# Weight assembly through PSUM, and a ring of two banks for both products of the feed-forward

## The chip, the cores and the metric

The kernel runs on one core of a Trainium2 chip. A core has TensorE (PE, matrix products into PSUM), VectorE (DVE), ScalarE (ACT), GpSimd (POOL) and the DMA queues, most of which SyncE (SP) issues to. PSUM has eight banks of 128 partitions x 512 fp32. The metric is the device time of one execution in microseconds; lower is better.

## The reference, cut to what matters

```python
# attention: B=4, H=8, S=576, D=64; only the 32 largest scores of a row are kept
scores = q @ k.T / sqrt(64)
kth    = np.partition(scores, -32)[..., -32]
attn   = softmax(where(scores >= kth, scores, -1e9))
x      = concat_heads(attn @ v)                       # 2304 tokens x 512
# feed-forward: w_in 512 x 2048, w_out 2048 x 512
h = x @ w_in
g = where(h > 0, h, exp(min(h, 0)) - 1)
y = g @ w_out
# experts: each token goes to the one of 8 whose embedding is most alike
e   = argmax(normalised(y) @ normalised(expert_emb).T / tau)
out = gate * (relu(y @ w1[e]) @ w2[e])
```

## The kernel before

**Stages.** `attention_and_ffn` does the attention, the feed-forward and the choice of the expert for all 2304 tokens; it ends at about 930 us of the trace. Then the experts follow one by one. The change touches the first part alone.

**Tiles and slots.** A tile is 128 query rows of one head (or 64 rows of two heads for the last rows of a batch); there are 144, in the order of `tiles`. Eight of them, all heads of the same 128 tokens, make a slot; there are 18 slots. A tile goes through: scores on PE into one of two `sc` banks pairs (L781), a copy by ACT into one of five `arena` buffers of a pair of tiles (L787), the search for the 32nd largest score on DVE (L676 to L708; L703 reads the `sc` bank again and so frees it), masking and exponentials on ACT and POOL (L806 to L825), a transposing DMA (L827) and the product with v on PE into the one `acc` bank (L857). After the last tile of a slot, L889 on DVE divides by the row sums, from `acc` into one of three `rr` buffers, and a DMA turns the slot's tokens into `xt`.

**Feed-forward of a slot** (`ffn_ops`, L908). The 2048 hidden columns are done in four units of 512. A unit has 48 products of 128 columns into the bank `hp` (L916 to L918), an exponential and a relu on ACT into an `rr` buffer (L938, L939), L940 on DVE, which reads `hp` and `rr`, and two copies of the result as fp16 high and low part into a buffer `gt` (L943 or L945, L946). Then come 12 products of 512 columns from `gt` into the bank `y` (L923 to L925), which collects all four units. `hp` and `y` have one bank each, `gt` has two buffers. When all is in `y`, ACT copies it out (L962), and `route_ops` finds the expert.

**Weights** (`weights`, L1105). w_in and w_out are read as halves of eight pieces each, 32 halves in all (`w_piece`, L468). Every number of a half is put together on DVE as an integer in three operations over 512 columns: c0 (L481) keeps and shifts one word into `fi`, a view of the final place in SBUF; c1 (L484) ors the sign and exponent bits of the same word into `fi`; c2 (L487) ors the shifted other word into `fi`. c1 and c2 so read two SBUF operands, the loaded words with a step of two, and `fi`. ACT sums the squares (L490), `pow2` makes a scale, and `w_split` (L499) splits each piece into a high and a low fp16 part: for w_in ACT and POOL, for w_out ACT (L507) and DVE (L512). The last piece of w_out lies in a buffer of its own, `wl`.

**Order.** A planner (`Plan`, L69) writes the order of each engine's instructions down ahead of time. Each operation has a guessed length, a due time counted in tiles, and the buffers that it reads and writes; a `Ring` hands out buffers in turn, and a ring with `in_order` only in the order in which they were asked for. The planner goes through simulated time and always puts the operation with the earliest due time next among those that can start. On the chip each engine keeps that order and waits on semaphores. First products of a unit are due at `d`, second products at `d + 2.4`; each set is cut into four operations:

```python
r_h = ring(ps, [128, 512], F32, "hp", 1)
r_y = ring(ps, [128, DM], F32, "y", K["yb"])
r_gt = ring(ff, [128, 2, 4, 128], F16, "gt", K["gt"])
d = d0 + (d1 - d0) * f / (NFB // 4)
for i in range(0, 4, n):
    FIRST["last"] = op("pe", 645 * n, d + K["f15"], lambda i=i: f2(gt, f, i, i + n), ...)
```

The bank `misc` is one as well; the transposes of q and k, `pow2` and `route_ops` use it.

Of the kernel before, what the change touches and what calls it, by code (L numbers as in the profile page):

```python
# [29 lines left out]
K = {'WD': 2.5, 'wa': 0.7, 'ws': 6.0, 'wsa': 0.6, 'wo': 6.0, 'wos': 13.0, 'wsp': (1, 1, 1, 1, 1, 1, 1, 1, 0, 0, 0, 0, 0, 0, 0, 0), 'kd': 5, 'qd': 7, 'vs': 1.3, 'va': 0.25, 'vp': -5.0, 'u': 20, 'cut': 4, 'ff0': 7, 'ffd': 7.0, 'rr': 3, 'nj': (3, 1), 'big': 3, 'kt': 4, 'wt': 0.4, 'wf': 0.9, 'vpo': 0, 'gth': 2, 'a4': (0, 20, 1), 'hp': 2, 'yb': 1, 'sc': 3, 'xt': 2, 'xsp': 0, 's': 5, 'w': 1, 'gt': 2, 'qraw': 1, 'dsc': 3.5, 'dcp': 2.0, 'dsg': 0.2, 'drl': 1.0, 'de': 1.0, 'dex': 0.8, 'dhi': 0.8, 'dlo': 0.9, 'dav': 3.5, 'dno': 3.5, 'drt': 2.0, 'f3': 0.3, 'f6': 0.6, 'f9': 0.9, 'f15': 2.4, 'ffs': 0.0, 'ct': 0.4, 'we': 0, 'wd0': -2.9, 'ahead': 4}  # L30
# [159 lines left out]
def topk_attention_ffn_experts_kernel(  # L190
# [160 lines left out]
    def attention_and_ffn(fast):  # L351
# [116 lines left out]
        def w_piece(t, tb, i, src, st, stb, due, far=()):  # L468

            f = wview(t, i, 2)  # L470
            k = src.shape[1] // 2
            for h in range(2):
                d = far[(2 * i + h) % len(far)] if far else r_big()
                fh = f[:, h * 512:(h + 1) * 512]
                fi = fh.bitcast(I32)
# [20 lines left out]
                if h:
                    op("act", 1040, due + 1, sq, r=[tb[i + 1]], w=[d, stb])

        def w_split(t, tb, i, sb, due, pool):  # L499
# [408 lines left out]
        def ffn_ops(c, d0, d1):  # L908
            xt, y = xts[c], r_y()
# [10 lines left out]
            def f2(gt, f, i0, i1):  # L920
                for i in range(i0, i1):
                    fb = 4 * f + i
                    nc.tensor.matmul(y.t, gt.t[:, 0, i, :], wo_at(0, fb), start=(fb == 0), stop=False)  # L923
# [111 lines left out]
        def first_expert():  # L1035
# [463 lines left out]
```

## Time and profile before

| | |
|---|---|
| median of 3 runs | 1254.1 us (1249.03 to 1255.2) |
| profiled execution, device time | 1257.39 us |
| its span, first to last instruction | 1255.6 us |
| mean granted TensorE clock | 0.913 |
| busy in the span | PE 83%, DVE 69%, ACT 68%, POOL 62% |
| DMA | 165.85 MB, 132 GB/s mean |

Times in the rows are counted from the first instruction of the span. The device time is 1.8 us longer than the span. Busy shares are means over stages that differ, so the rows below take the stages one by one. Matmuls overlap each other, and a product's length in the trace is its latency; how fast PE goes is read from the distance of two starts. The granted clock is a share of 2.4 GHz.

### The profile page before, as it was taken

How to read it: one execution, taken by the hardware profiler on the slowest of the kernel's cores; microseconds unless marked ns; L12 is line 12 of the kernel's file. 1: busy time of each engine (PE TensorE's matmuls, PEld its weight loads, DVE VectorE, ACT ScalarE, POOL GpSimd, SP SyncE). 2: the span in 40 equal slices, each digit the busy share in tenths (PEclk: the TensorE clock that was granted, in tenths of full speed). 3: DMA queues.
4: the chain of work that ended last, by engine and by line, in shares of the span. 5: the costliest groups of instructions: out<-in, count | busy, mean ns of one | idle time of the engine just before them, and what ended most of it. 6: DMA issues, size and time to landing. Idle time of an engine off the chain costs nothing. (4 is left out here: it accounts for less than half of the span.)

```text
span 1255.6 us, 28591 instructions
## 1 busy us (share of the span) xinstructions
PE 1036.1 (83%) x10112; PEld 799.0 (64%) x10112; DVE 865.1 (69%) x3588; ACT 847.8 (68%) x1807; POOL 780.8 (62%) x816
## 2 busy tenths in 40 slices
PE   4565537899798999798898988998887788998996
PEld 2354426666566777576676666776664677777785
DVE  4789999988798988789887898886213244434310
ACT  3687878889788989878887888876233244444421
POOL 1267979887688988678886788988313234323300
PEclk9957757999899999989998988999898889999998
DMA  7997633746764757945756674434407455455400
GB/s 202 303 235 192 161 93 71 144 94 149 161 122 100 125 107 156 167 81 102 126 95 127 146 145 85 90 77 89 136 11 228 143 184 185 134 163 178 142 20 16
DMA packets 321732, 165.85 MB, mean 132 GB/s; under 512 B 257990, under 2 KB 298054, under 8 KB 321552
## 3 DMA queue, kind: packets, MB, share of 16 engines
q1 hardware_dynamic: 316816, 150.67, 52.1%
q0 software_dynamic: 4736, 12.92, 3.4%
q8 instruction: 95, 1.56, 0.6%
q14 instruction: 85, 0.70, 0.2%
HBM read 77.43 MB, written 11.40 MB: 71 GB/s over the span
## 5 line engine op out<-in xcount | busy, mean ns | idle before, releaser
L916 PE MATMUL hp<-xt,ww 128*128 128x128 f16 x1152 | 216.8, 229 | 25.0 <-DVE rr L940 22.8
L917 PE MATMUL hp<-xt,ww 128*128 128x128 f16 x1152 | 216.7, 229 | 0.0
L918 PE MATMUL hp<-xt,ww 128*128 128x128 f16 x1152 | 216.4, 229 | 0.0
L816 POOL TENSOR_TENSOR arena<-arena,k 128x576 f32<-128x576 f32 x144 | 191.4, 1330 | 37.6 <-ACT k L806 36.7
L825 POOL TENSOR_TENSOR php<-arena,php 128x576 f16<-128x576 f32 x144 | 188.0, 1306 | 6.5
L781 PE MATMUL sc<-arena_r,qd 128*128 128x288 bf16 (+1 forms) x960 | 145.5, 308 | 43.2 <-ACT arena L787 17.7
L676 DVE MAX8 cand<-arena 128x8 f32<-128x82 f32 (+1 forms) x1008 | 161.3, 229 | 26.1 <-ACT arena L787 25.2
L787 ACT ACTIVATE arena<-sc 128x288 f32<-128x288 f32 x288 | 113.5, 408 | 47.0 <-PE sc L781 45.4
L857 PEld LDWEIGHTS <-pt 128*128 128x128 f16 (+3 forms) x2400 | 99.7, 104 | 68.6 <-DMA pt<-php 36.3
L781 PEld LDWEIGHTS <-qd 128*128 128x128 bf16 (+1 forms) x960 | 86.7, 107 | 88.4 <-issue 44.7
L916 PEld LDWEIGHTS <-ww 128*128 128x128 f16 x1152 | 119.8, 104 | 27.1 <-DVE rr L940 15.3
L821 POOL TENSOR_SCALAR php<-arena 128x576 f16<-128x576 f32 x144 | 101.5, 705 | 47.4 <-ACT arena L818 44.3
L917 PEld LDWEIGHTS <-ww 128*128 128x128 f16 x1152 | 118.8, 103 | 17.1 <-issue 11.9
L691 ACT ACTIVATE k<-arena,mba 128x576 bf16<-128x576 f32 x144 | 111.4, 774 | 14.8 <-DVE mx L696 7.7
L806 ACT ACTIVATE k<-arena,mba 128x576 bf16<-128x576 f32 x144 | 111.7, 776 | 14.0 <-DVE mba L708 8.0
L818 ACT ACTIVATE arena<-arena,mx 128x576 f32<-128x576 f32 x144 | 111.6, 775 | 11.8 <-POOL arena L816 11.4
L918 PEld LDWEIGHTS <-ww 128*128 128x128 f16 x1152 | 119.0, 103 | 0.0
L857 PE MATMUL acc<-vb,pt 128*128 128x64 f16 (+1 forms) x1920 | 91.5, 201 | 32.7 <-DMA pt<-php 30.8
L925 PE MATMUL y<-ww,gt 128*128 128x512 f16 x288 | 109.2, 379 | 4.6 <-POOL gt L946 4.6
L707 DVE MAX8 w<-w 128x8 f32<-128x585 f32 x144 | 109.9, 763 | 4.1 <-POOL w L701 3.2
L923 PE MATMUL y<-ww,gt 128*128 128x512 f16 x288 | 109.5, 380 | 0.6 <-ACT gt L945 0.6
L924 PE MATMUL y<-ww,gt 128*128 128x512 f16 x288 | 109.1, 379 | 0.0
(300 smaller groups left out, 2747.1 us busy)
## 6 DMA issues: line engine op xcount, KB each, us to landing
arena<-in_moe_w_dram SPq DMA_DIRECT2D x52, 512.0 KB, 5.6
arena_r<-big SPq DMA_DIRECT2D x64, 144.0 KB, 2.6
big<-in_moe_w_out_dram SPq DMA_DIRECT2D x16, 512.0 KB, 4.6
ww<-in_moe_w_in_dram SPq DMA_DIRECT2D x14, 512.0 KB, 7.1
qd<-big SPq DMA_DIRECT2D x32, 192.0 KB, 2.9
ysc<-big SPq DMA_DIRECT2D x20, 258.0 KB, 4.8
w<-in_moe_w_dram SPq DMA_DIRECT2D x10, 512.0 KB, 12.4
big<-in_v_dram SPq DMA_DIRECT2D x9, 512.0 KB, 8.8
```

Of the source, the lines that this page charges most:

```text
L676: v.max(out=cand.t[:, 8 * g:8 * g + 8], in_=x()[:, ENDS[g]:ENDS[g + 1]])
L691: op("act", 760, n + K["dsg"], lambda: nc.scalar.activation(k.t(), x(), AF.Sign, scale=-1.0, bias=th.t, accum_out=ds.t), r=[sb, th, k.base ...
L781: nc.tensor.matmul(o[64 * g:64 * g + 64] if s is None else o, qd.t[:, i, g, p * n:p * n + n], kt.t[:, g, i // 2, cs], start=i == 0, stop=i ...
L787: op("act", 291, n - K["dcp"], lambda c=c: nc.scalar.activation(sb.t()[:, c * 288:c * 288 + 288], sc.t[:, SC0 + c * 288:SC0 + c * 288 + 28 ...
L806: op("act", 667, n + K["drl"], lambda: nc.scalar.activation(k.t(), sb.t(), AF.Relu, scale=-HUGE, bias=kb.t), r=[sb, kb, s2, k2], w=[k])
L816: op("pool", 1242, e, lambda sb_=sb_, k_=k_: nc.gpsimd.tensor_tensor(sb_.t(), sb_.t(), k_.t(), op=ALU.subtract), r=[k_, s2, k2], w=[sb_])
L818: op("act", 760, e + K["dex"], lambda sb_=sb_, mx_=mx_, i_=i_: nc.scalar.activation(sb_.t(), sb_.t(), AF.Exp, scale=scale, bias=mx_(), acc ...
L825: op("pool", 1270, e + K["dlo"], lambda sb_=sb_, i=i: nc.gpsimd.tensor_tensor(ph.t[:, i, 1, 0:S], sb_.t(), ph.t[:, i, 0, 0:S], op=ALU.subt ...
L857: nc.tensor.matmul(acc.t[out_, cs], t[h][rows, g, :], rhs, start=(i == 0), stop=(i == len(units) - 1))
L916: nc.tensor.matmul(hp.t[:, i * 128:i * 128 + 128], wi_at(0, kb, fb), xh, start=(kb == 0), stop=False)
L917: nc.tensor.matmul(hp.t[:, i * 128:i * 128 + 128], wi_at(0, kb, fb), xl, start=False, stop=False)
L918: nc.tensor.matmul(hp.t[:, i * 128:i * 128 + 128], wi_at(1, kb, fb), xh, start=False, stop=(kb == KB - 1))
```

## The change

**Assembly.** Each half takes a PSUM bank `x`, from the ring `hp` for w_in and from `misc` for w_out. c0 writes to `x`, c1 reads and writes `x`, and c2 reads `x` and writes the final place in SBUF. The planner's guesses go from 400, 700, 700 to 400, 600, 600 ns.

**Banks of the feed-forward.** The ring `y` goes, and `hp` has two banks. A slot takes five turns of that ring: four units, and then `y`. The second products of a slot are no longer put behind each unit but all together behind the fourth, due at the end of the slot's time (`d1`). So `gt` has four buffers: two as before, two as views of `wl`. The first copy into `gt` of each unit has to wait for the last split that reads `wl` (`done`).

```diff
@@ K @@
-'gt': 2
+'gt': 4
@@ rings @@
-        r_h = ring(ps, [128, 512], F32, "hp", 1)
-        r_y = ring(ps, [128, DM], F32, "y", K["yb"])
+        r_h = ring(ps, [128, 512], F32, "hp", 2)
...
-        r_gt = ring(ff, [128, 2, 4, 128], F16, "gt", K["gt"])
+        gts = [ff.tile([128, 2, 4, 128], F16, name=f"gt{i}", bufs=1) for i in range(2)]
+        gts += [wl.bitcast(F16)[:, i * 1024:i * 1024 + 1024].rearrange("p (a b c) -> p a b c", a=2, b=4) for i in range(2)]
+        r_gt = turns(4, lambda i: gts[i])
@@ w_piece @@
-                fh = f[:, h * 512:(h + 1) * 512]
-                fi = fh.bitcast(I32)
+                x = (r_h if t is wi else r_misc)()
+                fi = f[:, h * 512:(h + 1) * 512].bitcast(I32)
...
-                def c0(d=d, fi=fi):
-                    nc.vector.tensor_scalar(fi, d.t[:, 0:1024].bitcast(I32)[:, 1:1024:2], 0x07FFFFFF, 3, op0=ALU.bitwise_and, op1=ALU.logical_shift_left)
+                def c0(d=d, x=x):
+                    nc.vector.tensor_scalar(x.t.bitcast(I32), d.t[:, 0:1024].bitcast(I32)[:, 1:1024:2], 0x07FFFFFF, 3, op0=ALU.bitwise_and, op1=ALU.logical_shift_left)
-                def c1(d=d, fi=fi):
-                    nc.vector.scalar_tensor_tensor(fi, d.t[:, 0:1024].bitcast(I32)[:, 1:1024:2], -0x40000000, fi, op0=ALU.bitwise_and, op1=ALU.bitwise_or)
+                def c1(d=d, x=x):
+                    nc.vector.scalar_tensor_tensor(x.t.bitcast(I32), d.t[:, 0:1024].bitcast(I32)[:, 1:1024:2], -0x40000000, x.t.bitcast(I32), op0=ALU.bitwise_and, op1=ALU.bitwise_or)
-                def c2(d=d, fi=fi):
-                    nc.vector.scalar_tensor_tensor(fi, d.t[:, 0:1024].bitcast(I32)[:, 0:1024:2], 29, fi, op0=ALU.logical_shift_right, op1=ALU.bitwise_or)
+                def c2(d=d, x=x, fi=fi):
+                    nc.vector.scalar_tensor_tensor(fi, d.t[:, 0:1024].bitcast(I32)[:, 0:1024:2], 29, x.t.bitcast(I32), op0=ALU.logical_shift_right, op1=ALU.bitwise_or)
...
-                op("dve", 400, due, c0, r=[d], w=[tb[i + 1]])
-                op("dve", 700, due, c1, r=[d], w=[tb[i + 1]])
-                op("dve", 700, due, c2, r=[d], w=[tb[i + 1]])
+                op("dve", 400, due, c0, r=[d], w=[x])
+                op("dve", 600, due, c1, r=[d], w=[x])
+                op("dve", 600, due, c2, r=[d, x], w=[tb[i + 1]])
@@ w_split: the same operation, and done[:] = [it] @@
@@ get_q: the first q's bank @@
-            x, m, qn, qd, qx = r_qraw(), (r_misc if QT else r_y)(), r_big(), r_qd(), Buf(t=1)
+            x, m, qn, qd, qx = r_qraw(), (r_misc if QT else r_h)(), r_big(), r_qd(), Buf(t=1)
@@ ffn_ops @@
-            xt, y = xts[c], r_y()
+            xt, second = xts[c], []
...
-                    op("act", 520, d + K["f9"], lambda: nc.scalar.activation(gt.t[:, 0], v3(r.t), AF.Copy), r=[r], w=[gt])
+                    op("act", 520, d + K["f9"], lambda: nc.scalar.activation(gt.t[:, 0], v3(r.t), AF.Copy), r=[r], w=[gt], after=done)
...
-                for i in range(0, 4, n):
-                    FIRST["last"] = op("pe", 645 * n, d + K["f15"], lambda i=i: f2(gt, f, i, i + n), r=[gt] + wo_b[2 * f + i // 2:2 * f + (i + n + 1) // 2], w=[y])
+                second.append((gt, f))
 
             for f in range(NFB // 4):
                 unit(f)
+            y, n = r_h(), 4 // K["cut"]
+            for gt, f in second:
+                for i in range(0, 4, n):
+                    FIRST["last"] = op("pe", 645 * n, d1 + (f - 3) * .2, lambda gt=gt, f=f, i=i: f2(y, gt, f, i, i + n),
+                                       r=[gt] + wo_b[2 * f + i // 2:2 * f + (i + n + 1) // 2], w=[y])
@@ first_expert: two banks of hp in place of hp and y @@
-            up0(op, N + 60, x0, x, [r_h(), r_y()], late(0, 1024), Buf(t=1), raw, after=[FIRST["last"]])
+            up0(op, N + 60, x0, x, [r_h(), r_h()], late(0, 1024), Buf(t=1), raw, after=[FIRST["last"]])
```

## Rows read from the trace of the kernel before

**Rows 1.** Busy tenths of the page, 40 slices of 31.4 us: VectorE.

```profile
DVE  4789999988798988789887898886213244434310
```

**Rows 2.** Busy us by stretch: length, PE, PEld, DVE, ACT, POOL; clock, DMA share, GB/s.

```profile
150.00:200.00 50.00, 23.13 (x216) 16.89 (x214) 49.83 (x174) 39.01 (x74) 43.00 (x33) 0.62 0.33 83
400.00:500.00 100.00, 96.92 (x1162) 71.97 (x1160) 89.69 (x421) 91.17 (x214) 88.72 (x102) 1.00 0.59 118
```

**Rows 3.** Timeline of PE, second products of a slot: start us, length us.

```profile
889.04 0.38 PE L924 MATMUL y<-ww,gt 128*128 128x512 f16 x1
889.26 0.38 PE L925 MATMUL y<-ww,gt 128*128 128x512 f16 x1
```

**Rows 4.** Groups by line, DVE, 86 to 176 us: busy us, mean ns, idle before.

```profile
L484 DVE SCALAR_TENSOR_TENSOR ww<-big,ww 128x512 int32<-128x512 int32 x14 | 18.0, 1284 | 0.0
L487 DVE SCALAR_TENSOR_TENSOR ww<-big,ww 128x512 int32<-128x512 int32 x14 | 14.8, 1059 | 0.0
L481 DVE TENSOR_SCALAR ww<-big 128x512 int32<-128x512 int32 x14 | 12.9, 921 | 0.0
```

**Rows 5.** The same groups by line, DVE, 25 to 80 us.

```profile
L487 DVE SCALAR_TENSOR_TENSOR ww<-ww 128x512 int32<-128x512 int32 x14 | 12.9, 935 | 0.0
L484 DVE SCALAR_TENSOR_TENSOR ww<-ww 128x512 int32<-128x512 int32 x14 | 10.7, 782 | 0.0
L481 DVE TENSOR_SCALAR ww<-ww 128x512 int32<-128x512 int32 x14 | 9.0, 661 | 2.3 <-DMA ww<-in_moe_w_in_dram 2.3
```

**Rows 6.** One line each: count, ns least/median/most, first and last start us.

```profile
L484 DVE SCALAR_TENSOR_TENSOR ww<-big,ww x14: 672/1276/2480, 87.3 to 165.1; 128x512 int32<-128x512 int32 x14
L481 DVE TENSOR_SCALAR ww<-ww x14: 407/416/1498, 26.6 to 68.9; 128x512 int32<-128x512 int32 x14
L940 DVE SCALAR_TENSOR_TENSOR rr<-hp,sc,rr x4: 723/739/751, 188.7 to 221.9; 128x512 f32<-128x512 f32 x4
L703 DVE SCALAR_TENSOR_TENSOR w<-sc,mba,arena x115: 767/810/819, 234.6 to 849.1; 128x576 f32<-128x576 f32 x115
```

**Rows 7.** Groups by line, POOL: L816 in 86 to 176, then 230 to 850 us.

```profile
L816 POOL TENSOR_TENSOR arena<-arena,k 128x576 f32<-128x576 f32 x10 | 15.2, 1516 | 3.3 <-ACT k L806 2.9 <-ACT big L527 0.4
...
L816 POOL TENSOR_TENSOR arena<-arena,k 128x576 f32<-128x576 f32 x116 | 149.1, 1287 | 25.3 <-ACT k L806 24.7
```

**Rows 8.** One line each, as in rows 6: last weight split, first g, second slot's normalisation.

```profile
L512 DVE SCALAR_TENSOR_TENSOR ww<-wl,so,ww x1: 2261/2261/2261, 209.2 to 209.2; 128x1024 f16<-128x1024 f32 x1
L943 POOL TENSOR_SCALAR gt<-rr x18: 609/620/647, 189.5 to 907.3; 128x512 f16<-128x512 f32 x18
L889 DVE TENSOR_TENSOR rr<-acc,rinv x1: 667/667/667, 197.4 to 197.4; 128x512 f32<-128x512 f32 x1
```

**Rows 9.** Waits, 230 to 850 us: us in total, times, longest.

```profile
ACT arena L787 <- PE sc L781: 33.9, 39, 3.8
PE sc L781 <- DVE w L703: 6.9, 7, 1.5
PE hp L916 <- DVE rr L940: 6.7, 7, 1.6
```

**Rows 10.** Last slot: its stretch, then timelines of ACT and DVE (start, length us).

```profile
897.90:929.10 31.20, 27.52 (x253) 21.33 (x254) 4.69 (x14) 8.28 (x14) 6.87 (x9) 0.84 0.03 10
904.89 0.69 ACT L938 ACTIVATE rr<-hp,sc 128x512 f32<-128x512 f32 x1 [0.63 <-PE hp L918]
911.77 0.69 ACT L938 ACTIVATE rr<-hp,sc 128x512 f32<-128x512 f32 x1 [5.34 <-PE hp L918]
922.31 0.69 ACT L938 ACTIVATE rr<-hp,sc 128x512 f32<-128x512 f32 x1 [2.23 <-PE hp L918]
929.06 0.69 ACT L962 ACTIVATE big<-y,sc 128x512 f32<-128x512 f32 x1 [3.66 <-PE y L925]
906.46 0.75 DVE L940 SCALAR_TENSOR_TENSOR rr<-hp,sc,rr 128x512 f32<-128x512 f32 x1 [1.73 <-ACT rr L939]
918.61 0.75 DVE L940 SCALAR_TENSOR_TENSOR rr<-hp,sc,rr 128x512 f32<-128x512 f32 x1 [4.52 <-ACT rr L939]
```

More of the change, by code (lines that the diff above doesn't have):

```diff
@@ L29 @@
 ENDS = (0, 83, 166, 248, 330, 412, 494, 576)
-K = {'WD': 2.5, 'wa': 0.7, 'ws': 6.0, 'wsa': 0.6, 'wo': 6.0, 'wos': 13.0, 'wsp': (1, 1, 1, 1, 1, 1, 1, 1, 0, 0, 0, 0, 0, 0, 0, 0), 'kd': 5, 'qd': 7, 'vs': 1.3, 'va': 0.25, 'vp': -5.0, 'u': 20, 'cut': 4, 'ff0': 7, 'ffd': 7.0, 'rr': 3, 'nj': (3, 1), 'big': 3, 'kt': 4, 'wt': 0.4, 'wf': 0.9, 'vpo': 0, 'gth': 2, 'a4': (0, 20, 1), 'hp': 2, 'yb': 1, 'sc': 3, 'xt': 2, 'xsp': 0, 's': 5, 'w': 1, 'gt': 2, 'qraw': 1, 'dsc': 3.5, 'dcp': 2.0, 'dsg': 0.2, 'drl': 1.0, 'de': 1.0, 'dex': 0.8, 'dhi': 0.8, 'dlo': 0.9, 'dav': 3.5, 'dno': 3.5, 'drt': 2.0, 'f3': 0.3, 'f6': 0.6, 'f9': 0.9, 'f15': 2.4, 'ffs': 0.0, 'ct': 0.4, 'we': 0, 'wd0': -2.9, 'ahead': 4}
+K = {'WD': 2.5, 'wa': 0.7, 'ws': 6.0, 'wsa': 0.6, 'wo': 6.0, 'wos': 13.0, 'wsp': (1, 1, 1, 1, 1, 1, 1, 1, 0, 0, 0, 0, 0, 0, 0, 0), 'kd': 5, 'qd': 7, 'vs': 1.3, 'va': 0.25, 'vp': -5.0, 'u': 20, 'cut': 4, 'ff0': 7, 'ffd': 7.0, 'rr': 3, 'nj': (3, 1), 'big': 3, 'kt': 4, 'wt': 0.4, 'wf': 0.9, 'vpo': 0, 'gth': 2, 'a4': (0, 20, 1), 'hp': 2, 'yb': 1, 'sc': 3, 'xt': 2, 'xsp': 0, 's': 5, 'w': 1, 'gt': 4, 'qraw': 1, 'dsc': 3.5, 'dcp': 2.0, 'dsg': 0.2, 'drl': 1.0, 'de': 1.0, 'dex': 0.8, 'dhi': 0.8, 'dlo': 0.9, 'dav': 3.5, 'dno': 3.5, 'drt': 2.0, 'f3': 0.3, 'f6': 0.6, 'f9': 0.9, 'f15': 2.4, 'ffs': 0.0, 'ct': 0.4, 'we': 0, 'wd0': -2.9, 'ahead': 4}
 def pick(n, key):
@@ L415, in attention_and_ffn @@
         r_pw = ring(sm, [128, 4], F32, "pw", 1)
-        for r in [r_sc, r_s, r_k, r_php, r_pt, r_top, r_w, r_acc, r_xs, r_xt, r_h, r_gt, r_y]:
+        for r in [r_sc, r_s, r_k, r_php, r_pt, r_top, r_w, r_acc, r_xs, r_xt, r_h, r_gt]:
             r.in_order = True
@@ L511, in w_split @@
                 return
-            op("dve", 1196, due, lambda: nc.vector.scalar_tensor_tensor(lo, f, s, hi, op0=ALU.mult, op1=ALU.subtract),
-               r=[tb[i + 1], sb], w=[tb[i]])
+            done[:] = [op("dve", 1196, due, lambda: nc.vector.scalar_tensor_tensor(lo, f, s, hi, op0=ALU.mult, op1=ALU.subtract),
+               r=[tb[i + 1], sb], w=[tb[i]])]
         def wi_at(part, kb, fb):
@@ L519, in wo_at @@
             return wview(wo, fb // 2, part)[:, (fb % 2) * 512:(fb % 2) * 512 + 512]
-        KT, VB, QT, hold = {}, {}, {}, []
+        KT, VB, QT, hold, done = {}, {}, {}, [], []
         def thirds(x, m, first, due, dst, ns, reads):
@@ L918, in f1, with f2 @@
                         nc.tensor.matmul(hp.t[:, i * 128:i * 128 + 128], wi_at(1, kb, fb), xh, start=False, stop=(kb == KB - 1))
-            def f2(gt, f, i0, i1):
+            def f2(y, gt, f, i0, i1):
                 for i in range(i0, i1):
@@ L942, in unit @@
                 if (4 * c + f) * K["gth"] % 8 < K["gth"]:
-                    op("pool", 588, d + K["f9"], lambda: nc.gpsimd.tensor_scalar(gt.t[:, 0], v3(r.t), 1.0, 0.0, op0=ALU.mult, op1=ALU.add), r=[r], w=[gt])
+                    op("pool", 588, d + K["f9"], lambda: nc.gpsimd.tensor_scalar(gt.t[:, 0], v3(r.t), 1.0, 0.0, op0=ALU.mult, op1=ALU.add), r=[r], w=[gt], after=done)
                 else:
-                    op("act", 520, d + K["f9"], lambda: nc.scalar.activation(gt.t[:, 0], v3(r.t), AF.Copy), r=[r], w=[gt])
+                    op("act", 520, d + K["f9"], lambda: nc.scalar.activation(gt.t[:, 0], v3(r.t), AF.Copy), r=[r], w=[gt], after=done)
                 op("pool", 1113, d + K["f9"], lambda: nc.gpsimd.tensor_tensor(gt.t[:, 1], v3(r.t), gt.t[:, 0], op=ALU.subtract), r=[r], w=[gt])
-                for i in range(0, 4, n):
-                    FIRST["last"] = op("pe", 645 * n, d + K["f15"], lambda i=i: f2(gt, f, i, i + n), r=[gt] + wo_b[2 * f + i // 2:2 * f + (i + n + 1) // 2], w=[y])
+                second.append((gt, f))
             for f in range(NFB // 4):
                 unit(f)
+            y, n = r_h(), 4 // K["cut"]
[3 more added lines that the diff above has]
+                                       r=[gt] + wo_b[2 * f + i // 2:2 * f + (i + n + 1) // 2], w=[y])
             route_ops(c, y, d1 + K["drt"])
```

## The prediction

> **What bounds the kernel now.** I read the busy tenths of the page first. VectorE (DVE) stands at 7 to 9 from slice 2 to slice 27 (a slice is 31.4 us) and at 4 or less after slice 28, where the attention ends [rows 1]. Next comes the table by stretch: from 150 to 200 us DVE is busy 49.83 of 50 us, PE 23.13 at a granted clock of 0.62; from 400 to 500 us PE 96.92, ACT 91.17, DVE 89.69 and POOL 88.72 of 100 [rows 2]. PE's figure flatters: two second products start 0.22 us apart and last 0.38 each, so its busy time is no measure of room left [rows 3]. So the kernel has a start in which DVE is full and PE is not, a middle in which all are nearly full, and an expert part. The start is a DVE queue: what is taken off DVE there moves all later work forward, while the middle has no single owner.
>
> Third, what DVE does in its full stretch, 86 to 176 us: the three integer operations that assemble w_out, 18.0 + 14.8 + 12.9 us for 14 of 16 half-pieces, so 3.26 us each and about 52 us for 16, of 90 [rows 4]. For w_in (25 to 80 us) the same three cost 12.9 + 10.7 + 9.0 us for 14, 2.33 each, 37 us for 16 [rows 5]. The reason is in the spread: L484 ran at 672 ns least, 1276 median and 2480 most over w_out's pieces, whereas L940, which has as many elements but one operand in PSUM, took 723 to 751 just afterwards, and L703, also with a PSUM operand, 767 to 819 over the whole middle [rows 6]. POOL pays too: its subtraction L816 took 1516 ns in 86 to 176 us against 1287 later [rows 7]. DVE and POOL delay each other when DVE takes two SBUF operands, as L484 and L487 do.
>
> **The assembly through PSUM.** Nothing is added or dropped: 3 operations x 32 half-pieces stay. c1 and c2 keep one SBUF operand and get one from PSUM; c0 and c1 write to PSUM. The page "GPSIMD Engine Reference" of the Trainium skill (Specifications) says that POOL shares its SBUF interface with DVE instructions that have two SBUF inputs or run in a two-port mode; rows 6 agree.
>
> - c2 has exactly the pattern of L940: 0.74 us [rows 6].
> - c1 also writes PSUM, which no row shows for this size. Bounds: 0.67 (the SBUF form undisturbed) and 0.82 (the longest L703, 576 columns instead of 512) [rows 6]. I take 0.74, as L940 is nearest.
> - c0 undisturbed takes 407 to 416 ns [rows 6], faster than one element per cycle of its neighbours. Bounds 0.41 and 0.82 as above; I take 0.67, the undisturbed time of the one-element rate, because one end of it is now PSUM.
>
> The rule that speaks against the change is here: "VectorE: DVE Perf Modes" of the Trainium skill (Why PSUM operands drop a tier) says that an fp32 operation with a PSUM operand runs at one element per cycle. By it the fast c0 is lost, and the sum stays as it is below; were it not so, another 8 us would go. No row shows this operation into PSUM.
>
> Sum per half: 0.67 + 0.74 + 0.74 = 2.15 us (1.82 to 2.38). For w_out 3.26 - 2.15 = 1.11 us, x 16 = **17.8 us** off a saturated DVE (14 to 23). For w_in 2.33 - 2.15 = 0.18 x 16 = 2.9 us (-1 to 8); there part of the time goes to loads and short waits, and I count it as 0. I take 17 for both, a little less than the first, because the halves share one bank (below). POOL's shorter times in the same stretch are cover for DVE's gain, no separate term.
>
> Banks: w_in's halves use the two hp banks, idle at that time. w_out's use the one misc bank, which the q transposes and the scale of w_out also want. A half holds it for its three operations, which run on one engine anyhow; a q or k preparation can push a half back, but DVE then has tile work. Cost 0; at worst a few us, inside the lower bound above.
>
> **The wait on the weight split.** All first copies of g now wait for the last L512. That starts at 209.2 and takes 2.26 us, so it ends at 211.5; before, the first copy started at 189.5 [rows 8]. With the start 17 us shorter it is 194.5 against 172.5. Queued behind: the second products of slot 0, and, less visibly, the three rr buffers, which units 0 to 2 then hold; the normalisation of slot 1 (197.4 [rows 8], so 180) needs one, holds the only acc bank, and could be 14 us late. What hides it: DVE works at the front of the attention, and the outputs of a tile are due 3.5 tiles later; it is full anyhow. I take 0; without that cover it is up to 14 us.
>
> **The second hp bank and the second products at the end of a slot.** The work is the same: 4 x 48 first and 48 wide products per slot. What goes is PE's wait for L940 before the next unit: 6.7 us in 7 times over the 620 us of the middle, of which the other engines hide most; ACT's 33.9 us for scores is a much larger wait and remains [rows 9]. Gain in the middle between 0 and 7 us; I take 0. What is late next: y now takes a turn in the same ring, so five allocations per slot go over two banks, and unit 1 of the next slot waits until ACT has copied y out.
>
> At the end of the attention nothing covers the wait, and the last slot shows it. The last slot begins at 897.9 us at a clock of 0.84 and y is copied out at 929.06 [rows 10]. Now: unit 0's first products end at 904.9, L940 at 906.46 + 0.75 = 907.2, only then unit 1, done at 911.8 (4.6 us, below full clock); unit 3 takes from 919.4 to 922.3 (2.9 us) [rows 10]. After: unit 1 follows at once, 904.9 + 4.6 = 909.5; unit 2 needs only L940 of unit 0, 912.4; unit 3's bank is free at 909.5 + 2.3 = 911.8, so it ends at 915.3. Then 48 wide products x 0.22 [rows 3] = 10.6 us: 925.9, with g of unit 3 ready in time (its L940 ends 917.6, PE comes to it at 923.2). That is 3.2 us sooner; if unit 1 too runs in 2.9, 4.9. I take **4 us** (0 to 8).
>
> **The sum.** The profiled execution took 1257.4 us (its span 1255.6 and 1.8 around it), 3.3 above the median of 1254.1. 17 + 4 = 21 us less: 1236.4 by the profile, **1233** against the median. The rest of the program has no date of its own: each step waits for earlier steps, so a forward shift goes through to the end.
>
> **The rivals.**
>
> 1. *The middle shortens too.* PE's 6.7 us go with everything queued behind them, w_in's 2.9 come through, and c0 keeps its fast rate, (0.67 - 0.41) x 32 = 8: 1233 - 18 = 1215. For it: PE and DVE are both near 90% in 400 to 500 us [rows 2], where small jitters add up. Against it: the wait is small beside those for scores.
> 2. *The start's gain is given back.* c0 and c1 near 0.82, so 17 becomes 14, and slot 0's 14 us wait for rr stalls the back of the attention, which the middle cannot make up: 1254 - 4 = 1250. For it: DVE's 49.83 of 50 says nothing about whether the outputs, not DVE, end each stage. Against it: five pairs of score buffers lie between.
> 3. *Slower: the block of second products holds up the scores.* 16 pieces, 10.6 us of PE, now fall due together, and the scores of a tile can only begin when L703 has freed one of two sc banks (PE already waited 6.9 us for that [rows 9]). DVE has one tile in hand, some 5 us (the 115 L703 come one in 5.4 us [rows 6]); if the planned order puts more than that in front of a score, DVE stands still. Place: the join of two slots, 15 times. At 2.5 us each that is 38 us: 1233 + 38 = 1271. It decides from 1.4 us per slot (21 / 15). For it: the order is fixed ahead by estimated times. Against it: the products are cut in pieces and overdue scores are placed first.
>
> **How the numbers follow.** Forecast 0.61 (its own range 1222 to 1245), rival 1 0.14, rival 2 0.13, rival 3 0.12. Range 1212 to 1252: all of the forecast, most of rivals 1 and 2, none of 3. A difference under 0.5% (6.3 us) is no change for this measurement: faster than 1247.8 are the forecast, rival 1 and a quarter of rival 2, 0.78; same most of rival 2, 0.11; slower rival 3, 0.11.
>
> **What would show it.** L481, L484 and L487 at 0.67, 0.74 and 0.74 with little spread, and L816 near 1.29 us in the start: the first step. The last L512 some 17 us earlier, and every later eviction of y too: that the gain goes through. L889 of slot 1 not before the last L512: the rr wait. First products of units 0 and 1 of the last slot back to back: the tail. The prediction is wrong if the evictions of y lose the 17 us on the way, or if DVE's wait for scores grows at slot joins.

## The result and the profile after

The changed kernel takes 1232.3 us in the median of 4 runs (1226.75 to 1234.84) against 1253.0 for the kernel before. The ratio is 0.984, 95% interval 0.9814 to 0.9867. The profiled execution took 1234.8 us, its span is 1233.0, so the span is 22.6 us shorter. The interval leaves no doubt of a gain, though it is under 2%. Lines have moved: c0, c1, c2 are L485, L488, L491, the last split is L516, L676 is now L680, L703 is L707, L707 is L711, L781 and L787 are L785 and L791, L816 is L820, L889 is L893, L916 is L920, L938 and L940 are L942 and L944, L943 is L947, and the copy of y L962 is L970. In the experiments, one of the nine runs of e6_done23, the longest at 1246.2 us, counts as slow and is left out of its ratio.

The busy tenths of the page after, VectorE, 40 slices, now of 30.8 us:

```profile
DVE  4789898998779897798789889987113443334310
```

By stretch (length, then busy us of PE, PEld, DVE, ACT, POOL, then clock, DMA share, GB/s):

```profile
86.00:162.00 76.00, 44.88 (x472) 34.95 (x472) 69.61 (x268) 67.96 (x133) 61.58 (x49) 0.72 0.74 190
150.00:200.00 50.00, 25.75 (x230) 19.90 (x230) 47.05 (x191) 43.58 (x85) 44.18 (x37) 0.63 0.39 84
400.00:500.00 100.00, 94.95 (x1149) 71.19 (x1146) 88.51 (x423) 92.14 (x217) 84.21 (x97) 0.98 0.71 130
```

and the kernel before over its own stretch of the same work, the assembly of w_out:

```profile
86.00:176.00 90.00, 49.02 (x460) 37.10 (x459) 88.96 (x285) 70.23 (x139) 70.91 (x50) 0.69 0.68 166
```

DVE was busy 88.96 of 90 us there and is now busy 69.61 of 76: it has some room [rows 2]. The middle, 400 to 500 us, looks as before.

The three assembly operations, one line each (count, ns least/median/most, first and last start). The rows with misc as bank are w_out's, those with hp w_in's:

```profile
L485 DVE TENSOR_SCALAR misc<-big x16: 670/682/695, 87.1 to 158.7; 128x512 int32<-128x512 int32 x16
L485 DVE TENSOR_SCALAR hp<-ww x14: 671/686/695, 26.5 to 72.0; 128x512 int32<-128x512 int32 x14
...
L488 DVE SCALAR_TENSOR_TENSOR misc<-big,misc x16: 675/684/697, 88.7 to 160.0; 128x512 int32<-128x512 int32 x16
L488 DVE SCALAR_TENSOR_TENSOR hp<-ww,hp x14: 674/692/697, 27.2 to 72.8; 128x512 int32<-128x512 int32 x14
...
L491 DVE SCALAR_TENSOR_TENSOR ww<-ww,hp x14: 664/680/686, 28.4 to 73.5; 128x512 int32<-128x512 int32 x14
L491 DVE SCALAR_TENSOR_TENSOR ww<-big,misc x14: 656/677/686, 89.4 to 154.8; 128x512 int32<-128x512 int32 x14
```

No row is above 697 ns. Before, the same operations ran up to 2480 [rows 6]. All 32 halves took 88.0 us of DVE, summed over the trace, and now take 65.6, 2.05 per half.

POOL's subtraction in the same stretch (busy us, mean ns, idle):

```profile
L820 POOL TENSOR_TENSOR arena<-arena,k 128x576 f32<-128x576 f32 x9 | 11.5, 1282 | 5.3 <-ACT k L810 4.7 <-DVE pw L448 0.6
```

It is back at about its length of the middle [rows 7].

The last weight split, the first copies of g and the second slot's division, as in [rows 8]:

```profile
L516 DVE SCALAR_TENSOR_TENSOR ww<-wl,so,ww x1: 1284/1284/1284, 194.9 to 194.9; 128x1024 f16<-128x1024 f32 x1
...
L947 POOL TENSOR_SCALAR gt<-rr x18: 608/618/674, 197.9 to 890.7; 128x512 f16<-128x512 f32 x18
...
L893 DVE TENSOR_TENSOR rr<-acc,rinv x2: 676/679/682, 201.1 to 228.7; 128x512 f32<-128x512 f32 x2
```

The split ends at 196.2 us instead of 211.5, 15.3 sooner. The first L947 starts at 197.9, behind it. Of the two L893 the first belongs to the second slot: 201.1 us, later than before (197.4), though everything around it comes sooner.

Waits from 215 to 830 us (us in total, times, longest):

```profile
ACT arena L791 <- PE sc L785: 48.1, 36, 5.6
DVE cand L680 <- ACT arena L791: 20.5, 22, 4.3
PE sc L785 <- DVE w L707: 4.6, 7, 1.3
PE hp L920 <- DVE rr L944: 3.6, 3, 1.4
```

PE's wait for L944 before the next unit went from 6.7 to 3.6 us [rows 9]; ACT waits more for scores, 48.1 us against 33.9, and DVE waits 20.5 us for ACT's copies of them, twice as long as before (230 to 850 us):

```profile
DVE cand L676 <- ACT arena L787: 10.4, 18, 1.4
```

The last slot: its stretch, then ACT's timeline (start, length), with the copy of y of the slot ahead and of the last:

```profile
884.00:907.00 23.00, 22.89 (x245) 17.27 (x245) 3.00 (x4) 7.93 (x12) 5.24 (x5) 0.94 0.01 3
```

```profile
875.19 0.69 ACT L970 ACTIVATE big<-hp,sc 128x512 f32<-128x512 f32 x1 [6.81 <-PE hp L929]
888.31 0.69 ACT L942 ACTIVATE rr<-hp,sc 128x512 f32<-128x512 f32 x1 [6.75 <-PE hp L922]
890.93 0.69 ACT L942 ACTIVATE rr<-hp,sc 128x512 f32<-128x512 f32 x1 [1.09 <-PE hp L922]
893.82 0.67 ACT L942 ACTIVATE rr<-hp,sc 128x512 f32<-128x512 f32 x1
896.69 0.67 ACT L942 ACTIVATE rr<-hp,sc 128x512 f32<-128x512 f32 x1
906.73 0.69 ACT L970 ACTIVATE big<-hp,sc 128x512 f32<-128x512 f32 x1 [7.03 <-PE hp L929]
```

From the first L920 at 884.1 to the last L970 at 906.7 it takes 22.6 us; before it was 31.2 (897.9 to 929.06 [rows 10]). The exponentials come 2.6 to 2.9 us apart, where there were 6.9, 5.3 and 5.3.

**Three stages.** The sum can be read from three marks of each kernel: the end of the last weight split, the end of the last tile's search (last L707 or L711), and the last slot. The two rows of the second mark, before and after:

```profile
L707 DVE MAX8 w<-w x144: 746/762/772, 25.1 to 863.8; 128x8 f32<-128x585 f32 x144
```

```profile
L711 DVE MAX8 w<-w x144: 744/761/773, 25.4 to 850.2; 128x8 f32<-128x585 f32 x144
```

| | split ends | middle, to the last search | last slot | span |
|---|---|---|---|---|
| before | 211.5 | 653.1 | 31.2 | 1255.6 |
| changed | 196.2 | 654.8 | 22.6 | 1233.0 |

15.3 us came in the start, -1.7 in the middle, 8.6 in the last slot; the rest of the span differs by 0.4. At the split's end 20 of the 144 searches were done before and 21 are now (20 to 22 in all kernels below), so the first mark stands at nearly the same work. Each trace is one execution, and the timed executions of one kernel lie 2 to 17 us apart here: a single stage's difference of a few microseconds is not clear of that.

### The profile page after: what moved, and what is told of

Its sections match the earlier page's. It is cut to its first block, busy times and chain, and to the rows that moved or that the text cites. A ratio compares the mean times of both kernels' runs of the same rounds, so it can differ in the third digit from the quotient of the medians.

```text
span 1233.0 us, 28591 instructions
## 1 busy us (share of the span) xinstructions
PE 1028.0 (83%) x10093; PEld 789.9 (64%) x10093; DVE 842.7 (68%) x3588; ACT 845.8 (69%) x1807; POOL 767.8 (62%) x816
## 5 line engine op out<-in xcount | busy, mean ns | idle before, releaser
L920 PE MATMUL hp<-xt,ww 128*128 128x128 f16 x1152 | 206.8, 224 | 14.0 <-DVE rr L944 8.9
L820 POOL TENSOR_TENSOR arena<-arena,k 128x576 f32<-128x576 f32 x144 | 186.0, 1294 | 49.3 <-ACT k L810 47.8
L921 PE MATMUL hp<-xt,ww 128*128 128x128 f16 x1152 | 206.5, 223 | 0.0
L922 PE MATMUL hp<-xt,ww 128*128 128x128 f16 x1152 | 206.2, 223 | 0.0
L680 DVE MAX8 cand<-arena 128x8 f32<-128x82 f32 (+1 forms) x1008 | 161.5, 229 | 38.0 <-ACT arena L791 37.2
L785 PE MATMUL sc<-arena_r,qd 128*128 128x288 bf16 (+1 forms) x960 | 149.6, 316 | 41.5 <-ACT arena L791 16.8
L791 ACT ACTIVATE arena<-sc 128x288 f32<-128x288 f32 x288 | 113.2, 408 | 68.5 <-PE sc L785 66.5
L785 PEld LDWEIGHTS <-qd 128*128 128x128 bf16 (+1 forms) x960 | 87.2, 109 | 84.7 <-issue 38.3
L921 PEld LDWEIGHTS <-ww 128*128 128x128 f16 x1152 | 115.1, 100 | 12.3 <-issue 8.8
L920 PEld LDWEIGHTS <-ww 128*128 128x128 f16 x1152 | 115.7, 100 | 11.1 <-DVE rr L944 5.9
L825 POOL TENSOR_SCALAR php<-arena 128x576 f16<-128x576 f32 x144 | 97.6, 678 | 39.1 <-ACT arena L822 31.5
L922 PEld LDWEIGHTS <-ww 128*128 128x128 f16 x1152 | 115.2, 100 | 0.0
L711 DVE MAX8 w<-w 128x8 f32<-128x585 f32 x144 | 109.8, 763 | 2.7 <-POOL w L705 1.9
L707 DVE SCALAR_TENSOR_TENSOR w<-sc,mba,arena 128x576 f32<-128x576 f32 x124 | 100.6, 811 | 0.2
L690 DVE MAX8 top<-cand 128x8 f32<-128x56 f32 x432 | 89.2, 211 | 3.4
L1334 DVE SCALAR_TENSOR_TENSOR hl<-hp,hh 128x256 fp32r<-128x256 f32 x56 | 23.2, 422 | 97.5 <-ACT hh L1333 97.5
```

The source lines that it names most:

```text
L680: v.max(out=cand.t[:, 8 * g:8 * g + 8], in_=x()[:, ENDS[g]:ENDS[g + 1]])
L785: nc.tensor.matmul(o[64 * g:64 * g + 64] if s is None else o, qd.t[:, i, g, p * n:p * n + n], kt.t[:, g, i // 2, cs], start=i == 0, stop=i ...
L791: op("act", 291, n - K["dcp"], lambda c=c: nc.scalar.activation(sb.t()[:, c * 288:c * 288 + 288], sc.t[:, SC0 + c * 288:SC0 + c * 288 + 28 ...
L820: op("pool", 1242, e, lambda sb_=sb_, k_=k_: nc.gpsimd.tensor_tensor(sb_.t(), sb_.t(), k_.t(), op=ALU.subtract), r=[k_, s2, k2], w=[sb_])
L920: nc.tensor.matmul(hp.t[:, i * 128:i * 128 + 128], wi_at(0, kb, fb), xh, start=(kb == 0), stop=False)
L921: nc.tensor.matmul(hp.t[:, i * 128:i * 128 + 128], wi_at(0, kb, fb), xl, start=False, stop=False)
```

## The experiments

Each was timed beside the kernel before on the same chip, and not all on one chip. Ratios are to that kernel, so two experiments are compared by their ratios; the 95% interval stands in brackets.

**Assembly alone (e1_assembly).**

```diff
 r_h = ring(ps, [128, 512], F32, "hp", 1)     # as before, and r_y, two gt buffers, f2 behind each unit
+x = (r_h if t is wi else r_misc)()           # c0, c1, c2 and their guesses as in the change
```

> The kernel before with the assembly in PSUM alone (hp for w_in, misc for w_out; one hp bank, one y bank, two gt buffers, second products behind each unit as before). Theory (the gain is DVE time in the start, which passes through to the end): the three operations near 0.68 us each as in the changed kernel, the last split of w_out 12 to 17 us earlier than at 209 us, the last slot still 29 to 33 us long, time 1235 to 1240, so 13 to 18 us less than before. Rival (the feed-forward's order carries the gain and the start's time is given back in the middle): 1246 to 1253.

1225.7 us (1222.9 to 1226.9), ratio 0.981 (0.9778 to 0.9842): 24.7 us less than the kernel before, more than either theory said. Whether it is faster than the whole change (0.9814 to 0.9867) is not clear, since the intervals overlap. Its last split and its last search:

```profile
L513 DVE SCALAR_TENSOR_TENSOR ww<-wl,so,ww x1: 1750/1750/1750, 196.1 to 196.1; 128x1024 f16<-128x1024 f32 x1
...
L708 DVE MAX8 w<-w x144: 747/762/772, 25.0 to 835.8; 128x8 f32<-128x585 f32 x144
```

and ACT's timeline of its last slot:

```profile
874.25 0.69 ACT L939 ACTIVATE rr<-hp,sc 128x512 f32<-128x512 f32 x1
881.12 0.69 ACT L939 ACTIVATE rr<-hp,sc 128x512 f32<-128x512 f32 x1 [5.34 <-PE hp L919]
898.42 0.69 ACT L963 ACTIVATE big<-y,sc 128x512 f32<-128x512 f32 x1 [3.66 <-PE y L926]
```

The start (197.9) and the last slot (30.6 us) are as the theory had them. The surprise is the middle: 836.6 - 197.9 = 638.7 us, 14 less than before, with the feed-forward of the kernel before.

**Feed-forward alone (e2_ffn).**

```diff
 r_h = ring(ps, [128, 512], F32, "hp", 2)     # and all else of ffn_ops as in the change
-x = (r_h if t is wi else r_misc)()           # w_piece and its guesses as before
```

> The changed kernel with the old assembly in SBUF: two hp banks, four gt buffers, second products together, but w_piece and its guesses as before. Theory: the last slot lasts 22 to 25 us instead of 31, all else as before, time 1245 to 1249. Rival (the feed-forward's order carries the gain): 1233 to 1240. Second rival (the block of second products costs the middle more than the tail gives): 1253 or more, with more wait for scores in the middle than before.

1236.7 us (1233.3 to 1243.7), ratio 0.990 (0.9863 to 0.9937). The last slot, first products from 894.4:

```profile
899.76 0.69 ACT L941 ACTIVATE rr<-hp,sc 128x512 f32<-128x512 f32 x1 [6.80 <-PE hp L921]
902.38 0.69 ACT L941 ACTIVATE rr<-hp,sc 128x512 f32<-128x512 f32 x1 [1.08 <-PE hp L921]
918.19 0.69 ACT L969 ACTIVATE big<-hp,sc 128x512 f32<-128x512 f32 x1 [7.02 <-PE hp L928]
```

23.8 us, as expected. The time lies in the first rival's range, not in the theory's; in the trace, an execution of 1243.7 us, the middle too is 4.9 us shorter, 648.2 us. The two parts alone save some 25 and 14 us; together they save 21. So the parts don't simply add. In the traces the start and the last slot nearly add (13.6 and -1.7 alone, 15.3 together; 0.6 and 7.4, 8.6 together); most of what doesn't is the middle (14.4 and 4.9, -1.7 together).

**True guesses (e4_true_guess).** `c0 400 -> 685, c1 600 -> 687, c2 600 -> 678` in the changed kernel.

> The changed kernel with the planner told what the chip takes: 685, 687, 678 ns for the three operations instead of 400, 600, 600. Theory (the shorter operations are the gain, the order is second): within 5 us of 1232. Rival (the planner's guess, nearer to the truth than before, is part of the gain): a further 5 to 15 us less, 1217 to 1227, through a better order in the first 200 us.

1224.3 us (1222.3 to 1234.8), ratio 0.983 (0.9785 to 0.9868). The number is the rival's, but the ratio can't be told from the changed kernel's 0.984, and the rival's reason is not borne out: the split ends at 200.1 us, 4 later than in the changed kernel. The middle is 639.5.

**The wait for wl only where wl is used (e6_done23).**

```diff
-r=[r], w=[gt], after=done)
+r=[r], w=[gt], after=done if f > 1 else [])
```

> The changed kernel, but only units 2 and 3 of a slot, whose gt buffers lie in wl, wait for the last split; units 0 and 1 do not. The second slot's division L893, at 201 us in the changed kernel since rr was held, should come at 180 to 190. Theory (the rr wait costs nothing at the end, since the front of the attention has work): within 3 us of 1232. Rival (that delay costs its 10 to 20 us somewhere later): 1215 to 1225.

1237.6 us (1227.2 to 1246.2), ratio 0.990 (0.9866 to 0.9941). The second slot's division is the first of these two:

```profile
L893 DVE TENSOR_TENSOR rr<-acc,rinv x2: 675/678/680, 184.5 to 224.4; 128x512 f32<-128x512 f32 x2
```

184.5 us instead of 201.1, and nothing was gained; the time is 3 us above the theory's range. The wait exists, and no gain from its going shows at the end. But this edit changes the written order as well, which moves the time by as much as the rival's 10 to 20 us (below), so a smaller cost of the wait is not excluded.

**A nudge (e7_nudge).** `op("dve", 400, due, c0, ...)` becomes 410 in the changed kernel. On every engine the written order differs over long stretches; operations, buffers and waits for data are the same.

> The changed kernel with one guess of the planner 10 ns larger (c0 410 instead of 400), which moves the order of many instructions on every engine but no operation's length, buffer or count. From the end of the weight split to the last tile's L711 (the middle) the changed kernel took 654.8 us, the kernel before 653.1, assembly alone 638.7, and the changed kernel with true guesses 639.5. Theory (the middle's length is a matter of the written order, not of the change's parts): the middle again differs from 654.8 by 5 us or more, anywhere from 638 to 662, while the start (to 196 to 200 us) and the last slot (23 to 25 us) stay. Rival (the two hp banks and the block of second products cost the middle some 15 us, and true guesses remove that): 652 to 658, and 1230 to 1236 in all.

1224.0 us (1219.5 to 1228.4), ratio 0.979 (0.9756 to 0.9828). Last split and last search:

```profile
L516 DVE SCALAR_TENSOR_TENSOR ww<-wl,so,ww x1: 1285/1285/1285, 195.9 to 195.9; 128x1024 f16<-128x1024 f32 x1
...
L711 DVE MAX8 w<-w x144: 745/762/772, 25.1 to 841.7; 128x8 f32<-128x585 f32 x144
```

The middle is 842.5 - 197.2 = 645.3 us, 9.5 less than in the changed kernel, and the last slot 22.6 as there. By the ratios the ten nanoseconds in a guess moved the time by some 6 us, and the two intervals still overlap. That is the theory's number, and the rival's 652 to 658 is missed; the next runs show the order's weight beyond noise.

**The old guesses (e3_old_guess).** `c1 600 -> 700, c2 600 -> 700` in the changed kernel.

> The changed kernel with the old guesses (400, 700, 700). Theory (order, not parts): start 195 to 200 us, last slot 23 to 25 us, middle anywhere from 638 to 662. Rival (a guess nearer to the chip's 685 each gives a better order): between the changed kernel and the one with true guesses, 1224 to 1232, middle 640 to 650.

1218.5 us (1214.8 to 1221.7), ratio 0.975 (0.9711 to 0.9779): start 194.8, middle 647.8, last slot 23.3. This is clear of the changed kernel (0.9814 to 0.9867), with the same operations. It is lower than the rival's range. 700 is nearer to the chip's 685 than the change's 600, as the rival has it, but the kernel with the true guesses is slower than this one (0.9785 to 0.9868): fit of the guesses is not by itself what makes an order good.

**The kernel before with true guesses (e5_before_true_guess).** `c0 400 -> 775, c1 700 -> 988, c2 700 -> 988`.

> The kernel before with the planner told what its three operations took in the mean, 775, 988 and 988 ns, and nothing else. Theory (the start is bound by DVE's real lengths, which a guess cannot change): the weight split still ends at 208 to 216 us, the last slot lasts 30 to 33 us, and only the middle moves, by up to 15 us either way: 1238 to 1262. Rival (much of the assembly's gain is the better fitting guess): the split ends by 203 us, and 1232 to 1240.

1273.2 us (1271.2 to 1278.8), ratio 1.018 (1.0148 to 1.0216). Its last split:

```profile
L512 DVE SCALAR_TENSOR_TENSOR ww<-wl,so,ww x1: 1267/1267/1267, 217.9 to 217.9; 128x1024 f16<-128x1024 f32 x1
```

The split ends at 219.2, somewhat later than the theory's 216, the middle takes 660.8, and the time is above the theory's 1238 to 1262. The rival's direction is wrong: truer guesses alone make this kernel some 23 us slower. No operation differs, so this is the order, and far beyond noise. DVE's wait for score copies in its middle (219 to 880 us) is more than twice that of the kernel before:

```profile
DVE cand L676 <- ACT arena L787: 25.2, 24, 5.1
```

**Assembly alone, with the scores' bank in the last slot (e8_assembly_tail).**

```diff
-hp, r, gt = r_h(), r_rr(), r_gt()
+hp, r, gt = r_sc() if c == NSLOT - 1 and f % 2 else r_h(), r_rr(), r_gt()
...                                            # and hp.t[:, 0:512] where the bank is read
```

> Assembly alone (one hp bank, one y bank, second products behind each unit), and in the last slot alone units 1 and 3 take a bank of the scores, which is free by then. Theory (the second bank is worth its tail, 8 us, and nothing else is needed for it): the last slot 23 to 26 us instead of 31.3, and 1216 to 1220, if the order ahead of the last slot stays as in assembly alone, under both kernels. Rival (the last slot is bound by PE or by its low clock, and the shorter tail of the changed kernel came from the second products at the end): 29 us or more, 1224 to 1228.

1218.1 us (1215.6 to 1221.1), ratio 0.974 (0.9709 to 0.9775), faster than the kernel before and the changed one. ACT's timeline of the last slot, first products from 867.7:

```profile
874.70 0.69 ACT L939 ACTIVATE rr<-hp,sc 128x512 f32<-128x512 f32 x1 [0.67 <-PE hp L919]
878.17 0.69 ACT L939 ACTIVATE rr<-sc,sc 128x512 f32<-128x512 f32 x1 [1.94 <-PE sc L919]
881.52 0.69 ACT L939 ACTIVATE rr<-hp,sc 128x512 f32<-128x512 f32 x1 [0.37 <-PE hp L919]
883.59 0.69 ACT L939 ACTIVATE rr<-sc,sc 128x512 f32<-128x512 f32 x1 [0.54 <-PE sc L919]
893.89 0.69 ACT L963 ACTIVATE big<-y,sc 128x512 f32<-128x512 f32 x1 [4.50 <-PE y L926]
```

26.2 us against 30.6 in assembly alone, a little over the theory's range: the second bank by itself is worth 4.4 us, not 8. The exponentials now come 3.5, 3.4 and 2.1 us apart. Another 3.6 us lie between this and the changed kernel's 22.6, and 2.8 of them in unit 0. Here, as before, the routing of the slot ahead is carried out between its products, and from its first product to its exponential it takes 7.0 us. In the changed kernel y of the slot ahead was copied out at 875.2, 9 us before the last slot's first product, the routing is done before it, and unit 0 takes 4.2. The stretch of unit 0 and the eight products of the routing, first in the kernel before, then in the changed one (clock is the third number from the right):

```profile
897.90:904.90 7.00, 6.91 (x58) 6.82 (x59) 1.68 (x10) 0.36 (x3) 0.58 (x3) 0.52 0.00 0
899.18 1.82 PE L970 MATMUL misc<-ent,rr 128*128 128x8 f32 x8
884.10:888.40 4.30, 4.29 (x55) 4.29 (x55) 0.00 (x0) 0.09 (x1) 0.00 (x0) 0.69 0.01 1
878.27 1.06 PE L978 MATMUL misc<-ent,rr 128*128 128x8 f32 x8 [1.34 <-ACT rr L1005]
```

So some 1.8 us of unit 0's 2.8 are the routing, and the rest, about 1 us, goes with the clock: 0.52, almost wholly the low level of 1.2 GHz, before; 0.69 after. In both PE had stood idle just ahead, 1.7 and 3.2 us, waiting for the slot's tokens.

**c2 with two SBUF inputs (e9_c2_sbuf).**

```diff
-c1: x = (d & sign bits) | x        c2: fi = (d' >> 29) | x
+c1: fi = (d & sign bits) | x       c2: fi = (d' >> 29) | fi
```

> The changed kernel, but c1 writes its result to the final place in SBUF and c2 reads it from there: c1 has one PSUM input, c2 two SBUF inputs, both write SBUF. Theory (two SBUF inputs are what POOL and DVE fight over): over w_out's 16 halves c1 stays within 0.66 to 0.72 us, c2 spreads from 0.67 to over 1.6 with a mean near 1.05 as in the kernel before; the last half then ends 4 to 8 us later than at 161.5 us, and the start is that much longer. Rival (writing to SBUF while POOL writes is what costs): c1 spreads as c2 does. Second rival (POOL's load in this stretch happened to be lower in the changed kernel): neither spreads.

1234.6 us (1232.8 to 1235.2), ratio 0.985 (0.9818 to 0.9876). c1 and c2 over w_out:

```profile
L488 DVE SCALAR_TENSOR_TENSOR ww<-big,misc x14: 657/680/686, 90.0 to 159.8; 128x512 int32<-128x512 int32 x14
...
L491 DVE SCALAR_TENSOR_TENSOR ww<-big,ww x14: 677/971/1735, 90.7 to 160.5; 128x512 int32<-128x512 int32 x14
```

c1 writes to SBUF and stays within 30 ns; c2 reads two SBUF operands and spreads from 677 to 1735, as L487 did before. The two stand in one kernel, in the same stretch and in turn, so POOL's load is much the same for both. The last half ends 7.1 us later than in the changed kernel (168.6 against 161.5) and the split 6.6 later (202.8). So reading two operands from SBUF makes the operation spread, and writing there does not. That POOL is the other side can be read from the trace of the kernel before: of its 96 assembly operations, 42 ran with no POOL instruction beside them, and none of these took over 694 ns (c0 at most 427); each of the 32 that took over 750 ns had POOL at work for 65% of its length or more. In the time of the whole kernel the 6.6 us do not show: 0.985 and the changed kernel's 0.984 can't be told apart.

**The same with the old guesses (e10_tail_old_guess).** `c1 600 -> 700, c2 600 -> 700` in e8_assembly_tail.

> Assembly alone with the scores' bank for units 1 and 3 of the last slot, as before, and the guesses 400, 700, 700: the same operations in another order. Theory (the start and the last slot add to whatever the middle gives): w_out done by 155 to 163 us, last slot 26 to 28 us, middle 638 to 660, so 1215 to 1240. Rival (the guesses 400, 700, 700 give a better order of the middle, as the 1218.5 of the changed kernel with them suggests): middle under 638 and 1205 to 1214.

1229.3 us (1223.0 to 1240.3), ratio 0.982 (0.9781 to 0.9863): split at 194.8, middle 650.4, last slot 25.4. The old guesses, good in e3_old_guess, are 11 us worse here (10 by the ratios, whose intervals do not meet). The traced execution, 1223.7 us, is one of the shorter ones of this kernel.

**All together** (us of the profiled executions; rest is the span less the three stages; medians of the timed runs last):

| | split ends | middle | last slot | rest | span | median |
|---|---|---|---|---|---|---|
| before | 211.5 | 653.1 | 31.2 | 359.8 | 1255.6 | 1250 to 1253 |
| before, true guesses | 219.2 | 660.8 | 31.6 | 365.5 | 1277.1 | 1273.2 |
| assembly alone | 197.9 | 638.7 | 30.6 | 357.2 | 1224.4 | 1225.7 |
| feed-forward alone | 213.2 | 648.2 | 23.8 | 356.7 | 1241.9 | 1236.7 |
| changed | 196.2 | 654.8 | 22.6 | 359.4 | 1233.0 | 1232.3 |
| changed, nudge | 197.2 | 645.3 | 22.6 | 357.6 | 1222.7 | 1224.0 |
| changed, true guesses | 200.1 | 639.5 | 22.8 | 360.0 | 1222.4 | 1224.3 |
| changed, old guesses | 194.8 | 647.8 | 23.3 | 352.3 | 1218.2 | 1218.5 |
| changed, wait for wl in two units | 197.8 | 658.0 | 22.9 | 350.7 | 1229.4 | 1237.6 |
| changed, c2 from SBUF | 202.8 | 653.5 | 23.3 | 353.8 | 1233.4 | 1234.6 |
| assembly, scores' bank in the last slot | 195.4 | 640.4 | 26.2 | 356.3 | 1218.3 | 1218.1 |
| the same, old guesses | 194.8 | 650.4 | 25.4 | 351.3 | 1221.9 | 1229.3 |

The rest is the stretch from the last search to the last slot (29.5 to 36.1 us) and the experts after it (319.9 to 330.1). It too differs, by up to 14.8 us, though the experts' operations are the same in all but for the banks of the first. So the middle is not the whole of what an order moves: of the 14.8 us of span between the changed kernel and the same with the old guesses, 7.0 lie in the middle and 7.1 in the rest.

## Why the prediction was right

It said 1233; 1232.3 was measured. The first column of the table falls with the assembly alone, the third with the feed-forward alone, and the second and fourth follow neither. The two mechanisms are the ones forecast. That the sum came within a microsecond is luck: the changed kernel's operations under four sets of guesses took 1218.5 to 1232.3, and those of the kernel before under other guesses 1273.2.

- **What bounds the start.** Right. DVE was the queue, and POOL's interference with two-operand reads the reason for the long c1 and c2; e9_c2_sbuf shows it with one operation moved. c0, which reads one operand, ran at up to 2342 ns beside POOL too, and at no more than 427 without it. "GPSIMD Engine Reference" of the Trainium skill (Specifications) says that POOL's SBUF interfaces are shared with DVE, with contention where a DVE instruction has two SBUF inputs or runs in a 2-port mode. By the spread of c2 in e9_c2_sbuf, 677 to 1735 ns, the trace agrees.
- **The assembly's price.** Forecast 2.15 us per half, measured 2.05. c0 0.68 (0.67 taken), c1 0.68 and c2 0.68 (0.74 taken from L940, which is not quite the same pattern: it is fp32 and takes its factor from SBUF; which of the two makes it longer no run shows). The fast form of c0 is gone: 682 ns where 416 was the median over w_in's pieces [rows 6]. "VectorE: DVE Perf Modes" of the Trainium skill (Why PSUM operands drop a tier) says that an operand in PSUM rules out the mode that uses both SBUF read ports, which leaves fp32 at one element per cycle. 682 against 416 ns agrees, here for int32. Over w_out's pieces nothing was lost by it: with POOL at work there, c0's mean had been 921 ns [rows 4].
- **What of it comes through.** Forecast 17, measured 15.3 at the end of the split. 22.4 us left DVE's sum; 12.9 of them show at the last half (174.4 to 161.5), and two or three more in the splits behind it. The rest turned into idle time of DVE, which is busy 69.6 of 76 us now: once the queue is no longer full, DVE waits, 3.5 us of it for w_out's loads. Counting w_in's share as 0 was the right choice in effect. That the shift goes through to the end, as the prediction has it, is only roughly so: the copies of y, its own sign, come 14.7 us sooner in the first slot, 1.7 in the eighth and 22.3 in the last; assembly saved 25 us alone but 4 to 8 on top of the new feed-forward, and e9_c2_sbuf gave 6.6 us of the start back at no cost that shows.
- **The wait for wl.** Forecast at 0, with the division of the second slot up to 14 us late. It came at 201.1, 19 us after where a plain shift would put it, and no cost can be seen: e6_done23 brings it to 184.5 without gain, as far as its other order allows to say. Rival 2 had c0 and c1 near 0.82 besides; they are at 0.68.
- **The middle.** Forecast 0, measured +1.7, but the reason given was incomplete, and the hit here is luck. The work of the middle is not bound by any one engine, and its length depends on the written order: 638.7 to 660.8 us over these kernels, 7.0 and 10.0 us for other guesses alone in e3_old_guess and e10_tail_old_guess. The order of the changed kernel happens to give nearly the length of the kernel before. Rival 1 (a shorter middle) is what three other orders of the same operations gave, 1218 to 1224; e6_done23 gave a longer one. Rival 3 (the block of second products holds up the scores) has some support: DVE's wait for score copies, which the prediction named as a sign of being wrong, doubled from 10.4 to 20.5 us, and its longest, 4.3 us, falls at 517 us inside such a block (496.2 to 522.4), at the slot whose y comes only 1.7 us sooner. But the same block gave middles of 639.5 and 645.3, and the kernel before with true guesses, which has no such block, waits longer still, 25.2 us. So it is not a price of the block as such.
- **The last slot.** Forecast 4, measured 8.6; this term was mis-sized. The prediction's path gives 3.2. Against it unit 0 took 4.2 us instead of 7.0, unit 1 2.6 instead of 4.6, units 2 and 3 the 2.9 forecast, and the wide products 10.0 instead of 10.6: 3.2 + 2.8 + 2.0 + 0.6 = 8.6. The second bank gave 4.4 by itself (e8_assembly_tail against assembly alone), within the 3.2 to 4.9 worked out. Units 0 and 1 I had taken over from before, with the routing of the slot ahead in unit 0 and both at a low clock (0.52 in unit 0); in the changed kernel that routing lies ahead of them, and the clock is 0.69 in unit 0 and 0.94 over the slot.

Start 1.7 less than forecast, middle 1.7 worse, last slot 4.6 more: 15.3 - 1.7 + 8.6 = 22.2 of the 22.6 us of span.

What stays open: which places of the order make a middle, or the rest, long or short, and how much of a shorter start comes through under a given order. Over the twelve middles DVE's idle time differs by 29 us (69 to 98) and its busy time by 15 (555 to 570); its waits shift between ACT's sign and copy operations from one order to the next, and no single wait accounts for it in these traces.

## What to carry to other kernels

Where GpSimd works beside VectorE, look at the spread of VectorE's operations, not the mean alone: a form that runs at 0.68 us at best and 1.3 us in the median is paying for a neighbour, and one operand moved to PSUM can be cheaper than a faster mode. In a kernel whose order is written ahead from guessed lengths, change a guess or two and time that too, before 10 or 20 us in a balanced stage are put down to an edit. A second accumulation bank pays where nothing else covers the chain behind the first, which here is the last slot alone.

## What the runs showed of the hardware

- Over w_out's halves, the two-operand integer operation with both inputs in SBUF took 672 to 2480 ns (L484) before; with one input in PSUM 656 to 697. Undisturbed, the two forms are equal (L484 at least 672 ns, L488 675, for 512 columns). Over the whole trace before, no assembly operation without a POOL instruction beside it took more than 694 ns.
- c0 (L481), with one SBUF input and its output in SBUF, is disturbed as well: it took 405 to 427 ns without POOL and up to 2342 beside it; into PSUM 670 to 695.
- The interference is mutual: POOL's L816 (now L820) fell from 1516 to 1282 ns in the mean in the same stretch, as far as POOL's spans, which are rough in the profile, tell. The length of the last split, which reads two SBUF operands in every kernel, is chance in this: 2261 ns before and 1284 in the changed kernel, but 1267 in the kernel before with true guesses and 1750 in assembly alone.
- Writing the result to PSUM or to SBUF makes no difference to such an operation: c1 took 684 ns in the median into PSUM and 680 into SBUF.
